# Attention with mixed heads and a gated feed-forward: gathers of score rows issued three places ahead instead of two

## The chip, the cores and the metric

One core of one Trainium2 chip runs the program. The metric is the device time of one execution in microseconds (us); for the kernel before there are three timed runs, and one more execution was recorded by the hardware profiler. All stretches named below are in us from the start of the profiled span.

## What is computed

Eight batches, 12 heads, 448 tokens, head size 64. The scores of all heads are mixed by a 12 x 12 matrix before the softmax, the weights are mixed by another behind it, and the result goes through a feed-forward stage with a gate. Cut to what matters:

```python
scores = scale * np.matmul(q, k.transpose(0, 1, 3, 2))        # (8, 12, 448, 448)
scores = np.einsum('bhij,hg->bgij', scores, w_pre)            # mix of heads
scores = scores - np.max(scores, axis=-1, keepdims=True)
attn = np.exp(scores)
attn = attn / (np.sum(attn, axis=-1, keepdims=True) + 1e-09)
attn = np.einsum('bhij,hg->bgij', attn, w_post)               # mix of heads
x = np.matmul(attn, v)                                        # to (8 * 448, 768)
h = x @ w_in                                                  # 768 -> 2048
out = (h - np.tanh(h)) @ w_out                                # 2048 -> 768
```

## The kernel before

**Blocks, groups, places.** A batch's 448 tokens are cut into blocks of 120, 120, 120 and 88 rows, 32 blocks in all. A block is cut into groups of 10 tokens or fewer, so that 10 tokens of 12 heads make up to 120 rows; there are 360 groups. Two groups make a *place* of the attention stage, of which there are 180, numbered from 0. The loop over places is at line 1256.

**What a place does on TensorE (PE), in this order.** `premix(p)` (line 910) mixes the heads of the scores of the place's two groups: eight matmuls at L918. Then come the place's *jobs* (below). Then `mix(p - 1)` (line 945), 32 matmuls at L957 that mix the heads of the softmax of the place before; they read `wr`, the mixing matrix divided by the row sums. `wr(p - 1)` comes from a chain over four engines: VectorE (DVE) takes the maximum (L927), ScalarE (ACT) the exponential with its sum (L929, twice), DVE the reciprocal (L938, L939, in `norm`, line 933), GpSimd (POOL) the product (L940). PE cannot go past `mix(p - 1)` before POOL has made that `wr`. (The counts are the profile's; the order below prints half of them, x4, x16 and x24 for L918, L957 and L999, since each of these matmuls runs as two.) ACT copies the result of a mix (`at`, L967 or L974) at the start of the next place.

**The gathers.** A block's scores lie in a tile `s` with a token to a partition. `gather(t)` (line 904) is a DMA on the SyncE queue (SP) that lays the rows of group `t` out as rows of `t`, one tile of a ring of `RT = 6`. At place p the loop issues the gathers of groups 2p + 4 and 2p + 5, those of place p + 2; the first four are issued ahead of the loop. A ring tile is free again once `premix` has read it.

**The jobs.** They prepare other blocks. `scores` (S below; line 864) makes two heads of a block's scores, 6 matmuls at L874 and two copies at L879, one on DVE and one on ACT; it comes in pairs, three pairs a block. `values` (V; line 987) multiplies three of six head pairs with v, 48 matmuls at L999. `prep_k` and `prep_q` (k, q; lines 806, 832) turn k and q by TensorE, split each into two parts on ACT (L825, L853) and DVE (L826, L855). A planner (lines 1153 to 1230) deals them out: the scores of the next block get a window of places from `lo` to `hi` (lines 1158, 1159) so that they are there before the first gather that reads them; values get a window of their own; `prep_k` takes the first place from four behind its load on that has no `prep_q` and not more than one scores job or two values jobs. Most places hold two S or one V; a place's jobs are sorted k, q, V, S.

**The conversion.** Beside this, the weights of the feed-forward are split into parts by `Convert` and `narrow_quad` (lines 35 and 72), 48 pieces in turn from place 7 on, a new one every three or four places, each in seven steps of one place. Its instructions stand at the head of a place on each engine, ahead of `norm` and so of `wr`. On POOL step 2 is one product (L84), step 4 two (L96, L97), step 5 some sums, step 6 a difference and a cast (L103, L105), step 7 another difference (L108). On DVE step 1 has L81 and L82, step 3 has L90, L91 and L94. In the second half of the pieces (`sums_out`, line 123, of `w_out`) the cast L105 waits for one more ACT product, L131, which stands on ACT behind the place's copy of `at`. Two pieces overlap, so a place can hold step 2 of one and step 6 of the one before.

**The DMA queue.** All loads, the gathers and the conversion's stores go out on SP in program order; `issue(6)` (line 769) sends up to six waiting entries a place behind the gathers. POOL issues DMAs only in the feed-forward stage, through a ring of descriptors in SBUF (`dynamic_dma_scratch_size`, line 1379).

The feed-forward follows from about 842 us on and is untouched but for that ring.

Of the kernel before, what the change touches and what calls it, by code (L numbers as in the profile page):

```python
# [150 lines left out]
def kernel_body(  # L151
# [11 lines left out]
    nc = tc.nc  # L163
# [72 lines left out]
    def open_ps_h():  # L236
        ff.ps_h = ctx.enter_context(tc.tile_pool(name="ps_h", bufs=2, space=PSUM, side="left"))
# [498 lines left out]
    with ExitStack() as st:  # L736
# [16 lines left out]
        blocks = [(b, m) for b in range(B) for m in range(NM)]  # L753
# [15 lines left out]
        def issue(most):  # L769
            for x in (queue, slow):  # L770
                while x and most and x[0][0] < place[0]:
                    send(x, nc.sync)
                    most -= 1
# [121 lines left out]

        RT = 6
        tq = [gp.tile([P, S], F32, name="t", tag=f"t{n}", bufs=1) for n in range(RT)]
        for x in tq:  # L900

# [2 lines left out]
        def gather(t, eng=nc.sync):  # L904
            i, g = groups[t]
            x = tq[t % RT]
            eng.dma_start(x[D - HP : D - HP + rows[t], :], sts[i][tokens[t].start : tokens[t].stop : tokens[t].step])
            tg[t] = x

        def premix(p):  # L910


            pss = [ps_p.tile([P, S], F32, name="ps_p", tag="ps_p") for _ in halves]
            ts = [tg.pop(2 * p + j) for j in range(2)]
            for j in (1, 0):
                for r in (1, 0):
                    k = slice(r * D, D + r * H * half_rows(2 * p + j)[r])
                    nc.tensor.matmul(pss[r][halves[j], :], wpre[k, :], ts[j][k, :], start=True, stop=True)  # L918
            return pss

        def expo(p, pss):
            zs = gp.tile([P, 3, 2], F32, name="zs", tag="zs")
            es = []
            for r, ps in enumerate(pss):

                mx = gp.tile([P, 1], F32, name="mx", tag="mx")
                nc.vector.tensor_reduce(out=mx, in_=ps, axis=AX.X, op=ALU.max, negate=True)  # L927
                e = gp.tile([P, S], F32, name="e", tag="e", bufs=4)
                nc.scalar.activation(e, ps, AF.Exp, bias=mx, scale=1.0, accum_out=zs[:, 0, r : r + 1])  # L929
                es.append(e)  # L930
            te[p] = [es, zs]

        def norm(p):
            zs = te[p][1]
            wr = gp.tile([P, 2, D], F32, name="wr", tag="wr", bufs=2)[:, :, :HP]
            for r in range(2):

                nc.vector.tensor_scalar_add(zs[:, 1, r : r + 1], zs[:, 0, r : r + 1], 1e-9)  # L938
            nc.vector.reciprocal(zs[:, 2], zs[:, 1])  # L939
            nc.gpsimd.tensor_mul(  # L940
                wr, wpost[:, :HP].unsqueeze(1).to_broadcast([P, 2, HP]), zs[:, 2].unsqueeze(2).to_broadcast([P, 2, HP])
            )
            te[p].append(wr)
# [203 lines left out]
        first = [t for t, (i, g) in enumerate(groups) if g == 0] + [NG, NG, NG]  # L1147
        todo = {p: [] for p in range(NPL + 8)}

        def at_place(p, *job):  # L1150
            todo[p].append(job)

        halved = []
        for i in range(len(blocks)):

            f0, f1, f2 = first[i : i + 3]
            if i + 1 < len(blocks):
                lo = max(0, (f0 - 1) // 2 - 1)
                hi = f1 // 2 - 3
                for x in range(0 if i else 1, 3):  # L1160
                    e = lo + 2 * x if lo + 4 <= hi else lo + (hi - lo) * x // 2
                    halved.append((e if i else x - 1, hi, "s", i + 1, x))
            for x in range(2):
                halved.append(((f1 - 1) // 2 + 2, f2 // 2 + 1 if f2 < NG else NPL + 7, "v", i, x))
        at_s, p, kind = {}, 0, None
# [22 lines left out]
        def held(p):  # L1188
            return [a for f, *a in todo[p] if f is scores]
# [11 lines left out]
        for i, (b, m) in enumerate(blocks):  # L1201
            p0 = first[i] // 2
            if i + 2 < len(blocks):
                p = at_s[i + 2, 0] - 1
# [5 lines left out]
                for hq in range(NP // 2):  # L1210
                    at_place(p0 + 4 + hq, load_v, b, hq)
        for b in range(1, B):
            p, o, done = first[blocks.index((b - 1, 1))] // 2 - 4, 0, []
            for hq in range(3):
                if hq == 2:

                    p = max(p, done[0] + 1)
                at_place(p, load_k, b, hq)
                o = max(p + 4, o + 1)
                p += 1  # L1220
                if hq > KB - 4:

                    o = max(o, end_s[blocks.index((b - 1, 3)), hq - 1 - (KB - 4)] + 1)
                for r in range(2):

                    while any(f is prep_q for f, *a in todo[o]) or 2 * len(held(o)) + sum(f is values for f, *a in todo[o]) > 2:
                        o += 1
                    at_place(o, prep_k, b, 2 * hq + r)
                done.append(o)
                assert o < at_s[blocks.index((b, 0)), hq], (b, hq)  # L1230
# [25 lines left out]
        for p in range(NPL + 3):  # L1256
            if mixed:
                mixed()
                mixed = None
            if 5 <= p < NPL + 1:  # L1260
                conv.place()
            place[0] += 1
            for t in (2 * p + 4, 2 * p + 5):
                if t < NG:
                    gather(t)
            issue(6)
            if p == NPL + 1:
                for f in start.pop(p):
                    f()
            if p < NPL:  # L1270
                ps = premix(p)
            if 1 <= p < NPL + 1:
                norm(p - 1)
            if p == NPL:
                for f in x0[1:]:
                    f()
            if p < NPL:
                expo(p, ps)
            if p > NPL:
                next(xq)  # L1280
                next(xq)
            for f, *a in todo[p]:
                f(*a)
            for f in sooner:
                f()
            sooner.clear()
            if 1 <= p < NPL + 1:
                mixed = mix(p - 1)
            for f in then + last:
                f()  # L1290
            then.clear()
            last.clear()
            if p == NPL - 3:
                conv.rest(now)
                early.close()
                open_early()
            if p == NPL - 1:
                early_ps.close()
                open_ps_h()
            for f in start.get(p, ()):  # L1300
                f()
            for _ in range(pieces.get(p, 0)):
                next(xl)
# [91 lines left out]
```

## Time and profile before

| | |
|---|---|
| three timed runs | 1706.41, 1708.94, 1719.01 us; median 1708.94 us |
| profiled execution | 1703.0 us, its span 1701.3 us |
| mean granted TensorE clock | 0.994 |
| attention, first `premix` to the last `mix` | about 25 to 842 us |
| DMA engines busy in the attention stage | 0.80 of the time |

The profile counts an engine busy while an instruction runs on it and names for each wait the engine or DMA whose signal came last. In rows of the timeline the columns are start, duration, engine, line, operation, output and inputs, and in brackets the idle time of the engine before it with the releaser. Only waits of the engine that sets the end cost time; in the attention stage that is PE, which is busy 97% of it, so the account is kept in PE's idle time and in the clock that it is granted.

### The profile page before, as it was taken

To read this page: it belongs to the slowest core of one execution; us is meant where nothing else is said; L and a number is where in the kernel's file an instruction comes from. 1 tells how busy PE (TensorE), PEld (TensorE's weight loads), DVE (VectorE), ACT (ScalarE), POOL (GpSimd) and SP (SyncE) were. 2 spreads that over 40 slices of the span, in tenths; PEclk is the share of its full clock that TensorE was granted. 3 is DMA by queue.
4 is the path that set the end of the run, shared out by engine and by line. 5 is a ranking of instruction groups with operands and counts; after the bars stand their busy time and mean duration, and the time that the engine had idled before them with its cause. 6 is when DMAs were issued, how large, how long until landed. Compare 5 with 4: busy or idle time off the path is not lost.

```text
span 1701.3 us, 41215 instructions
## 1 busy us (share of the span) xinstructions
PE 1660.1 (98%) x16068; PEld 1379.8 (81%) x16068; DVE 1231.3 (72%) x2119; ACT 1091.1 (64%) x1920; POOL 585.5 (34%) x798
## 2 busy tenths in 40 slices
PE   8999999999999899999999999999999999999999
PEld 6777777777777677677788888888888888989999
DVE  5777777878777777675497899868778867778432
ACT  5777777777777677676586777556667456666331
POOL 1466667666666666662100111101001101011100
PEclk9999999999999999999999999999999999999999
DMA  8879889898987979856589899989999989988993
GB/s 183 218 228 257 255 246 276 247 270 259 256 253 231 269 234 257 254 182 208 190 269 340 273 331 318 346 295 335 318 334 362 368 272 327 326 311 327 404 413 132
DMA packets 322290, 475.09 MB, mean 279 GB/s; under 512 B 105264, under 2 KB 255280, under 8 KB 322096
## 3 DMA queue, kind: packets, MB, share of 16 engines
q1 hardware_dynamic: 305660, 414.34, 75.5%
q0 software_dynamic: 16128, 57.68, 8.7%
q8 instruction: 128, 2.10, 0.5%
q14 instruction: 66, 0.54, 0.1%
q10 hardware_dynamic: 308, 0.43, 0.1%
HBM read 274.73 MB, written 120.59 MB: 232 GB/s over the span
## 4 chain that ended last, share of the span: by engine, by line
PE 72%; DMA 7%; DVE 7%; ACT 4%; issue 4%; POOL 4%; SPq 1%; POOLq 0%; ACTq 0%; DVEq 0%
PE ps_o L957 11%; PE ps_h L291 8%; PE ps_h L292 7%; PE ps_h L294 7%; PE ps_m L999 6%; PE ps_p L918 6%; PE y L534 6%; PE y L532 6%; PE y L533 6%; PE ps_q L874 4%; DMA t<-s 2%; DMA gl<-gs 2%; ACT e L929 1%; DVE mx L927 1%; PE y L504 1%
## 5 line engine op out<-in xcount | busy, mean ns | idle before, releaser
L957 PEld LDWEIGHTS ps_o<-wr,e 60*112 60x112 f32 (+1 forms) x5760 | 303.3, 175 | 46.1 <-POOL wr L940 31.9
L957 PE MATMUL ps_o<-wr,e 60*112 60x60 f32 (+1 forms) x5760 | 314.5, 259 | 16.1 <-POOL wr L940 14.6
L929 ACT ACTIVATE e<-ps_p,mx 128x448 f32<-128x448 f32 x360 | 224.8, 631 | 117.2 <-DVE mx L927 82.8
L927 DVE TENSOR_REDUCE mx<-ps_p 128x1 f32<-128x448 f32 x360 | 206.5, 615 | 109.1 <-PE ps_p L918 108.5
L967 ACT COPY at<-ps_o 112x960 f32<-112x960 f32 x156 | 154.3, 989 | 103.4 <-PE ps_o L957 102.9
L918 PE MATMUL ps_p<-t,wpre 60*64 60x448 f32 (+1 forms) x1440 | 182.4, 570 | 6.7 <-DMA t<-s 6.6
L999 PEld LDWEIGHTS ps_m<-at,vr 112*64 112x64 f32 x3072 | 147.6, 137 | 23.0 <-issue 7.7
L999 PE MATMUL ps_m<-at,vr 112*64 112x120 f32 (+1 forms) x3072 | 161.4, 262 | 1.1 <-DMA vr<-in_v_dram 0.9
L532 PE MATMUL y<-w,gh 128*128 128x384 f32 x448 | 151.2, 338 | 2.1 <-DMA w<-wo 1.6
L940 POOL TENSOR_TENSOR wr<-wpost,zs 128x120 f32<-128x120 f32 x180 | 70.0, 389 | 237.6 <-DVE zs L939 199.0
L533 PE MATMUL y<-w,gh 128*128 128x384 f32 x448 | 150.5, 336 | 0.0
L534 PE MATMUL y<-w,gl 128*128 128x384 f32 x424 | 143.4, 338 | 3.0 <-DVE gl L450 3.0
L874 PEld LDWEIGHTS ps_q<-kk,qh 64*120 64x120 f32 (+1 forms) x768 | 59.1, 174 | 82.0 <-issue 45.1
L874 PE MATMUL ps_q<-kk,qh 64*120 64x448 f32 (+1 forms) x768 | 121.8, 394 | 0.9 <-ACT kk L825 0.4
L879 DVE COPY s<-ps_q 120x448 f32<-120x448 f32 (+1 forms) x192 | 112.2, 614 | 9.8 <-PE ps_q L874 8.0
L669 POOL DMA_DIRECT2D gs<-gb x24 | 17.2, 717 | 291.6 <-DVE gb L668 291.6
L307 ACT ACTIVATE u<-h 128x1024 f32<-128x1024 f32 x56 | 59.5, 1063 | 74.4 <-DVE h L716 70.5
L879 ACT COPY s<-ps_q 120x448 f32<-120x448 f32 (+1 forms) x192 | 94.9, 538 | 7.1 <-PE ps_q L874 6.7
L647 POOL DMA_DIRECT2D gs<-ga x24 | 17.2, 716 | 230.0 <-DVE ga L330 222.9
L532 PEld LDWEIGHTS y<-w,gh 128*128 128x128 f32 x448 | 84.2, 188 | 7.2 <-issue 3.5
L533 PEld LDWEIGHTS y<-w,gh 128*128 128x128 f32 x448 | 84.1, 188 | 3.4
L534 PEld LDWEIGHTS y<-w,gl 128*128 128x128 f32 x424 | 79.6, 188 | 4.6 <-DVE gl L450 4.6
(372 smaller groups left out, 3971.3 us busy)
## 6 DMA issues: line engine op xcount, KB each, us to landing
t<-s SPq DMA_DIRECT2D x342, 210.0 KB
wa<-ss SPq DMA_DIRECT2D x96, 384.0 KB
w<-wo SPq DMA_DIRECT2D x43, 768.0 KB
gl<-gs SPq DMA_DIRECT2D x62, 512.0 KB
wa<-wi SPq DMA_DIRECT2D x72, 384.0 KB
w<-ts SPq DMA_DIRECT2D x35, 768.0 KB
gs<-gs POOLq DMA_DIRECT2D x24, 768.0 KB, 9.2
cr<-in_moe_w_in_dram SPq DMA_DIRECT2D x48, 256.0 KB
```

The costliest lines, as they stand in the source:

```text
L291: nc.tensor.matmul(ph, w[:, c, 0], xh, start=start and c == 0, stop=False, skip_group_check=True)
L532: nc.tensor.matmul(y, gh[:, tok], wh, start=first, stop=False, skip_group_check=True)
L533: nc.tensor.matmul(y, gh[:, tok], wl, start=False, stop=False, skip_group_check=True)
L534: nc.tensor.matmul(y, gl[:, tok], wh, start=False, stop=last, skip_group_check=True)
L874: nc.tensor.matmul(ps[:n, :S], qx[a, hp, :], kx[a, hp % 2], start=(x == 0), stop=(x == 2))
L879: eng(sts[i][:n, 2 * hp + j, :], ps[:n, :S])
L918: nc.tensor.matmul(pss[r][halves[j], :], wpre[k, :], ts[j][k, :], start=True, stop=True)
L927: nc.vector.tensor_reduce(out=mx, in_=ps, axis=AX.X, op=ALU.max, negate=True)
L929: nc.scalar.activation(e, ps, AF.Exp, bias=mx, scale=1.0, accum_out=zs[:, 0, r : r + 1])
L957: nc.tensor.matmul(ps[:CP, j, c * GP : (c + 1) * GP].rearrange("p (h i) -> p h i", i=GI)[:, :, r * GH : (r + 1) * GH], e[k, c * CP : (c + ...
L967: nc.scalar.copy(ats[i0][:, :, :, at : at + 2 * GI].rearrange("p c h (j i) -> p j (c h) i", j=2), ps[:CP, :, : NC * GP].rearrange("p j (x ...
L999: nc.tensor.matmul(pv[j * D : (j + 1) * D, r, :n], vt[:, j, c, :], ats[i][:, c, 2 * hp + j, :n], start=(c == 0), stop=(c == NC - 1),)
```

## The change

The ring gets eight tiles, and at place p the gathers of groups 2p + 6 and 2p + 7 go out, those of place p + 3; at place 0 four gathers go out, so that none is left out. The windows of the scores (`lo`, `hi`) and the loads of k move a place sooner, since a block's scores must now be complete a place sooner. The SBUF for two more tiles of 448 floats comes in part from POOL's descriptor ring, which is cut from 4096 to 2048 bytes a partition.

```diff
-        RT = 6
+        RT = 8
...
-                lo = max(0, (f0 - 1) // 2 - 1)
-                hi = f1 // 2 - 3
+                lo = max(0, (f0 - 1) // 2 - 2)
+                hi = f1 // 2 - 4
...
-            p, o, done = first[blocks.index((b - 1, 1))] // 2 - 4, 0, []
+            p, o, done = first[blocks.index((b - 1, 1))] // 2 - 5, 0, []
...
-            for t in (2 * p + 4, 2 * p + 5):
+            for t in range(2 * p + 6 if p else 4, 2 * p + 8):
                 if t < NG:
                     gather(t)
             issue(6)
...
-    nc = _bacc.Bacc("TRN2", target_bir_lowering=False, num_devices=1, dynamic_dma_scratch_size=4096)
+    nc = _bacc.Bacc("TRN2", target_bir_lowering=False, num_devices=1, dynamic_dma_scratch_size=2048)
```

No instruction is added but two MEMSETs of the new tiles (L902), which POOL runs at the start. The planner moves jobs between places, while the conversion stays at the same places: POOL's order is otherwise unchanged, and so is DVE's order of conversion steps against `norm`.

**PE, the k of the second load of a batch.** First the kernel before, places 17 and 18: `kr` is k as loaded, `kk` and `qh` the split k and q, `t` a ring tile, `ps_m`, `ps_q`, `ps_p`, `ps_o` PSUM tiles.

```order
L918 MATMUL ps_p<-t,wpre 64x448 x4
L814 MATMUL ps_m<-ident,kr 128x112 x8
L874 MATMUL ps_q<-kk,qh 120x448 x4
L874 MATMUL ps_q<-kk,ql 120x448 x2
L957 MATMUL ps_o<-wr,e 112x12x5 x16
L918 MATMUL ps_p<-t,wpre 64x448 x4
L874 MATMUL ps_q<-kk,qh 120x448 x4
L874 MATMUL ps_q<-kk,ql 120x448 x2
L957 MATMUL ps_o<-wr,e 112x12x5 x16
```

The same k in the changed kernel, places 16 and 17:

```order
L918 MATMUL ps_p<-t,wpre 64x448 x4
L814 MATMUL ps_m<-ident,kr 128x112 x8
L999 MATMUL ps_m<-at,vr 64x120 x24
L957 MATMUL ps_o<-wr,e 112x12x5 x16
L918 MATMUL ps_p<-t,wpre 64x448 x4
L874 MATMUL ps_q<-kk,qh 120x448 x4
L874 MATMUL ps_q<-kk,ql 120x448 x2
L874 MATMUL ps_q<-kk,qh 120x448 x4
L874 MATMUL ps_q<-kk,ql 120x448 x2
L957 MATMUL ps_o<-wr,e 112x12x5 x16
```

`prep_k` shared a place with one S and now shares one with V. Counted over PE's whole order within the loop, L814 is followed by scores in 10 places and by values in 11 before, and in 4 and 17 now. The places of the 10 are 17, 28, 40, 62, 73, 85, 107, 118, 130 and 152; of the 4 they are 5, 50, 95 and 140.

**ACT, the places with L131 directly ahead of L85** (step 6 of one piece of the second half beside step 2 of the next). There are five such places in each kernel, 99, 112, 125, 138 and 151. The second of them before, from the place's copy of `at` to the next place:

```order
L967 COPY at<-ps_o 112x2x48x10
L131 ACTIVATE ct<-ct 128x128
L85 ACTIVATE cr<-cr 128x512
L929 ACTIVATE e,zs<-ps_p,mx 128x448 x2
L974 COPY at<-ps_o 112x48x10
L974 COPY at<-ps_o 112x48x9
```

and in the changed kernel:

```order
L967 COPY at<-ps_o 112x2x48x10
L131 ACTIVATE ct<-ct 128x128
L85 ACTIVATE cr<-cr 128x512
L929 ACTIVATE e,zs<-ps_p,mx 128x448 x2
L879 COPY s<-ps_q 120x448
L974 COPY at<-ps_o 112x48x10
L974 COPY at<-ps_o 112x48x9
```

A copy of scores on ACT tells that the place now holds S where it held V (which leaves nothing on ACT). The five held, in their order, V with q, V, two S, V with q, two S; they now hold two S, S, S, two S, V with k.

## The prediction

> **What bounds the kernel now.** I read the busy time of the attention stage first, then PE's waits in it, then the timeline around each kind of wait.
>
> ```profile
> 25.20:842.00 816.80, 795.44 (x11596) 608.30 (x11596) 590.96 (x1502) 579.60 (x1329) 492.80 (x638) 0.99 0.80 240
> PE ps_o L957 <- POOL wr L940: 13.4, 16, 1.7
> PE ps_p L918 <- DMA t<-s: 6.6, 8, 1.6
> PE ps_m L999 <- DMA vr<-in_v_dram: 0.9, 1, 0.9
> ```
>
> The first row is the attention stage: 816.8 us, of them PE busy for 795.4 (the second number), DVE 591.0, ACT 579.6, POOL 492.8. PE sets the end, and only 21.4 us of the stage are left for any change of order to win. The other rows (us in total, times, longest) name nearly all of that: 6.6 us in which `premix` waited for its gathers, 13.4 us in which `mix` waited for POOL's `wr`. The change aims at the first, but it reorders the jobs that decide the second.
>
> **The gathers.** Why they are late shows on SP. The first rows are SP's own, the fifth is from the chain of waits, the last two are PE's.
>
> ```profile
> 155.91 1.62 SPq L907 DMA_DIRECT2D t<-s  x2
> 157.58 0.86 SPq L766 DMA_DIRECT2D kr<-in_k_dram  x1
> 158.61 6.68 SPq L766 DMA_DIRECT2D cr<-in_moe_w_in_dram  x2
> 165.39 1.65 SPq L907 DMA_DIRECT2D t<-s  x2
> 156.75 9.32 DMA t<-s
> 166.21 0.98 PE L918 MATMUL ps_p<-t,wpre 60*64 60x448 f32 x8 [0.93 <-DMA t<-s]
> 25.21 1.72 PE L918 MATMUL ps_p<-t,wpre 60*64 60x448 f32 x5 [1.65 <-DMA t<-s]
> ```
>
> A gather that went out at 156 took 9.32 us to land, and `premix` stood still for 0.93 us; SP itself hung for 6.68 us on two loads, so the next gathers were late too. A place lasts 816.8 / 180 = 4.54 us on average. Issued a place sooner, these gathers would have about 4.5 us more, against waits of under 1 us. The longest wait, 1.65 us, is that of place 0, whose gathers go out ahead of the loop as before; it stays. The gain is 6.6 - 1.65 = **-5.0 us**. SP sends the same DMAs in nearly the same mix, so what lies behind the gathers on its queue (loads with places to spare) is no later. The ring's own wait is the same too: with eight tiles the gather of place p + 3 needs the tile that `premix(p - 1)` read, as that of p + 2 did with six. A gather that opens a block still stands one place behind the last copies of its scores.
>
> The 0.9 us for `vr` is the last batch's v, read two places after its load; the values concerned now stand two places later (167 for 165), against a wait of 0.87 us: **-0.9 us**.
>
> **The k next to scores.** What PE loses to `wr` falls into kinds of places. The first kind is the place after `prep_k` and S.
>
> ```profile
> 100.01 1.16 DVE L826 TENSOR_TENSOR kk<-ps_m,kk 128x448 fp32r<-128x448 f32 x2 [0.46 <-ACT kk L825]
> 102.67 0.21 DVE L938 TENSOR_SCALAR zs<-zs 128x1 f32<-128x1 f32 x2
> 103.22 0.39 POOL L940 TENSOR_TENSOR wr<-wpost,zs 128x120 f32<-128x120 f32 x1 [3.54 <-DVE zs L939]
> 103.66 1.78 PE L957 MATMUL ps_o<-wr,e 60*112 60x60 f32 x32 [1.56 <-POOL wr L940]
> 153.33 1.78 PE L957 MATMUL ps_o<-wr,e 60*112 60x60 f32 x32 [0.99 <-POOL wr L940]
> 210.31 1.78 PE L957 MATMUL ps_o<-wr,e 60*112 60x60 f32 x32 [1.57 <-POOL wr L940]
> 358.31 1.79 PE L957 MATMUL ps_o<-wr,e 60*112 60x60 f32 x32 [0.65 <-POOL wr L940]
> 564.46 1.78 PE L957 MATMUL ps_o<-wr,e 60*112 60x60 f32 x32 [1.27 <-POOL wr L940]
> ```
>
> DVE is still at the split of k (1.16 us) when the place ends, then has step 3 of the conversion, and only then the reciprocal; `wr` is 1.56 us late. The five PE rows are the places after 17, 28, 40, 73 and 118, together 6.0 us. The other five such places (62, 85, 107, 130, 152) show no wait of this kind: no conversion step 3, or a place of two S behind, made the difference less. With V beside it a `prep_k` gives DVE 2.6 us more of PE time, and none of the 11 such places is followed by a wait. Now only four places hold k with S. Behind 51 and 96 there stand S and step 3, as in the two waits of 1.56 and 1.57, so I put 3.1 us there and nothing on the other two: -6.0 + 3.1 = **-2.9 us**. At places 18 and 41 two S with step 3 now follow two S; from nothing to half of the 1.56, I take 0.4 each, **+0.8 us**.
>
> **The conversion's cast next to scores.** This is the term that speaks against the change. In place 125:
>
> ```profile
> 589.64 0.98 ACT L967 COPY at<-ps_o 112x960 f32<-112x960 f32 x1
> 590.52 0.32 ACT L131 ACTIVATE ct<-ct 128x128 f32<-128x128 f32 x1
> 590.89 0.61 POOL L105 CAST ct<-ct 128x512 fp32r<-128x512 f32 x1 [1.61 <-ACT ct L131]
> 591.47 1.49 POOL L84 TENSOR_SCALAR cm<-cm 128x512 f32<-128x512 f32 x1
> 592.93 0.54 POOL L940 TENSOR_TENSOR wr<-wpost,zs 128x120 f32<-128x120 f32 x1
> 593.53 1.84 PE L957 MATMUL ps_o<-wr,e 60*112 60x60 f32 x32 [1.73 <-POOL wr L940]
> 719.56 1.78 PE L957 MATMUL ps_o<-wr,e 60*112 60x60 f32 x32 [1.62 <-POOL wr L940]
> 529.28 0.98 PE L918 MATMUL ps_p<-t,wpre 60*64 60x448 f32 x8
> 532.68 0.39 POOL L940 TENSOR_TENSOR wr<-wpost,zs 128x120 f32<-128x120 f32 x1
> 533.13 1.10 PE L957 MATMUL ps_o<-wr,e 60*112 60x60 f32 x18 [0.25 <-POOL wr L940]
> 590.35 0.63 PE L874 MATMUL ps_q<-kk,qh 64*88 64x448 f32 x4
> 591.43 0.37 PE L874 MATMUL ps_q<-kk,ql 64*88 64x448 f32 x2
> 688.05 1.79 PE L957 MATMUL ps_o<-wr,e 60*112 60x60 f32 x32 [0.62 <-POOL wr L940]
> ```
>
> The copy of `at` waits for the mix before; L131 stands behind it, POOL's cast waits for L131, the product L84 (1.49 us) follows, and `wr` comes last. So `wr` cannot be there sooner than some 3.85 us after the place's start (529.28 to 533.13 in place 112), whatever PE has to do. Place 112 holds V, which covers all but 0.25. Places 125 and 151 hold two S, done 2.3 us after the start: waits of 1.73 and 1.62. In 99 and 138, V with q covers it. One S (half of the two S of place 125, which run from 590.35 to 591.80, so 0.7 us, behind a `premix` of 0.9) is done at 1.6 and would leave 2.2. After the change 99 and 138 hold two S, 112 and 125 one S, 151 V with k: 2 x 1.7 + 2 x 2.2 = 7.8 us against 1.73 + 1.62 + 0.25 = 3.6, so **+4.2 us**. The bounds are nothing (were ACT's copy to come earlier) and 4 x 2.2 = 8.8 less 3.6.
>
> Without L84 in the place, the same chain made one S wait 0.62 us (688.05, place 145). S stands so at 119, 158 and 164 now, and at 145 no more: 3 x 0.62 - 0.62 = **+1.2 us**.
>
> **The clock.** Stalls of this length can cost twice.
>
> ```profile
> 591.71:595.12 3.41, 1.68 (x34) 1.59 (x32) 3.27 (x5) 1.74 (x6) 3.41 (x3) 1.00 1.01 242
> 595.12:598.53 3.41, 3.41 (x20) 1.78 (x18) 1.77 (x6) 1.70 (x5) 2.58 (x4) 0.50 0.88 293
> 718.00:721.41 3.41, 1.85 (x36) 1.79 (x40) 3.27 (x6) 1.54 (x6) 3.18 (x3) 1.00 0.87 281
> 721.41:724.82 3.41, 3.41 (x18) 1.74 (x18) 1.50 (x6) 2.05 (x4) 2.81 (x3) 0.50 1.11 262
> ```
>
> After 3.41 us with PE busy for 1.68 or 1.85 the next 3.41 us were granted half the clock (0.50), which costs up to 3.41 / 2 = 1.7 us. Both waits over 1.6 us did so, the waits of 1.56 and 1.57 did not. I expect three or four such drops in place of two, so 0 to +3.4, and take **+1.0**. The Trainium skill (TensorE: Matmul & The Clock Gate, "Why this matters for your kernels") wants no idle gaps of over about 3 us, a whole window, before the clock falls. By that rule no stall here would cost clock, this term would be 0 and the sum below -2.6 us; the trace disagrees, since 1.7 us of idleness within a window sufficed.
>
> **The smaller ring.** POOL's DMAs in the feed-forward:
>
> ```profile
> POOL gs L669 <- DVE gb L668: 291.6, 24, 16.5
> 957.29 0.75 POOL L670 DMA_DIRECT2D gs<-gs  x1
> 964.82 0.72 POOL L647 DMA_DIRECT2D gs<-ga  x1 [6.78 <-DVE ga L330]
> gs<-gs POOLq DMA_DIRECT2D x24, 768.0 KB, 9.2
> ```
>
> Three of them go out in some 18 us, each lands in 9.2 us or less, and POOL idles 6.8 us between them and 291.6 us for one line alone. Half a ring should hold what is in flight; should one DMA have to wait for an earlier one, POOL's idle time hides most of it. I take 0, with an upper end of 24 x (9.2 - 6.8) = 58 us. The Trainium skill (DMA: Bandwidth & Descriptors, "Terms") gives a descriptor 16 bytes, by which 2048 bytes make an estimated 128 descriptors an engine; no row here shows how many are in flight. The two added MEMSETs run on POOL while PE waits for the first loads: 0.
>
> **The sum.** -5.0 - 0.9 - 2.9 + 0.8 + 4.2 + 1.2 + 1.0 = -1.6 us. The same matmuls run, so PE's busy time stays. The profiled execution's 1703.0 becomes 1701.4; it lay 5.9 below the median of the timed runs, so for a median I forecast 1708.9 - 1.6 = **1707 us**: no change that a measurement tells (about 1%, 17 us, is what it can).
>
> **The rivals.**
>
> *Faster, 1699 us.* The gathers win their 5.0, and jobs that are spread more evenly (17 of the k beside V) remove the waits after k wholly, while the cast at the conversion costs as before, because ACT or POOL run ahead: -5.0 - 0.9 - 6.0 + about 2 = -10. For it: none of the 11 places of k with V was followed by a wait. Against it: the cast is bound to the mix before by L131, and POOL's order is fixed. If all 20 us of named waits but place 0's went, with two drops of the clock, the time would be 1709 - 22 = 1687.
>
> *Slower, 1718 us.* The cast next to scores decides: waits of 2.2 us at all of 99, 112, 125 and 138 (+5.2), 0.62 becoming 0.9 at the S without L84 (+2), the clock dropping after five stalls more (+8.5), less the 5.9 of gathers and v: +10. It is slower than before as soon as four drops are added. For it: both waits over 1.6 us halved the clock. Against it: where the stall lies across a window's edge it may not.
>
> *The gathers stay late*, 1712 us. If SP is held up by its loads for more than a place, as at 158.61 (6.68 us against 4.54), the extra place is used up and the 5.0 us are not won. Against it: waits of under 1 us need only that much more.
>
> *The ring stalls POOL*, 1730 us, some 20 of the 58 us.
>
> **Chances and range.** The forecast, within 6 us of 1707, 0.55; faster 0.18; slower 0.17; late gathers 0.06; the ring 0.04. The range runs from 1694 to 1719: it takes in the faster rival's middle and the slower one's, and leaves out its ends. Faster by over 1% (below 1692) needs nearly all waits gone: 0.06. Slower by over 1% (above 1726) needs the ring or more drops than I count: 0.07. Within 1%: 0.87.
>
> **What would show it.** In PE's waits `t<-s` falls from 6.6 us to about 1.7, the wait for `vr` goes; `wr` stays between 11 and 17 us, but at other places: waits of 1.6 us and more at the L957 that follow L131 and L84, at four places, most with S, one wait behind each of places 51 and 96, none after k with V. Windows at half clock stand behind the former. POOL's DMAs in the feed-forward keep 0.7 us. I am wrong if `t<-s` stays above 3 us, if `wr` falls below 8 us or rises above 22, or if the stage from 842 us on is more than 3 us longer.

## The result, and the profile after

Eleven runs of the changed kernel have a median of 1721.79 us (1715.43 to 1729.54), eleven of the kernel before on the same chip 1707.51 us (1702.51 to 1722.94): the ratio is 1.0072, 95% interval 1.0046 to 1.0098. The change costs some 12 us. The forecast was 1707, its range ended at 1719.

The profiled execution took 1726.18 us (span 1724.5, granted clock 0.986) against 1703.0 (1701.3, 0.994), 23.2 us more. The stretches first: of the changed kernel the attention stage and the feed-forward (columns as in the prediction's first row).

```profile
26.40:864.90 838.50, 810.40 (x11596) 617.00 (x11596) 592.23 (x1503) 581.66 (x1329) 493.98 (x638) 0.97 0.79 236
864.90:1724.50 859.60, 842.59 (x4328) 753.50 (x4328) 629.95 (x593) 501.77 (x573) 87.69 (x132) 1.00 0.89 318
```

The feed-forward before:

```profile
842.00:1701.30 859.30, 844.25 (x4328) 755.29 (x4328) 629.13 (x594) 501.70 (x573) 85.96 (x132) 1.00 0.89 319
```

The feed-forward has its old length (859.6 for 859.3). The attention stage is 838.5 - 816.8 = 21.7 us longer, and the busy column says of what kind: the same 11596 matmuls kept PE busy for 810.4 us in place of 795.4, so **15.0 us are slower matmuls**; PE's idle time went from 21.4 to 28.1, so **6.7 us are waits**. The remaining 1.2 us lie ahead of the first `premix`.

PE's waits in the attention stage of the changed kernel (us in total, times, longest):

```profile
PE ps_o L957 <- POOL wr L940: 26.1, 29, 2.2
PE ps_m L814 <- DVE s L879: 1.7, 2, 1.3
PE ps_p L918 <- DMA t<-s: 1.6, 1, 1.6
```

The gathers are there: 6.6 us have become the 1.6 of place 0, and the wait for `vr` is gone. But `wr`, 14.6 us over the same stretch before (the prediction's 13.4 stop at 842 us and leave out one wait of 1.16 us at the last mix, which both kernels have), is at 26.1, and a kind of wait that did not exist is there too (L814 for copies of scores).

Next the clock. These are windows of the changed kernel behind places 112, 138 and 158; the number behind POOL's is the granted clock.

```profile
546.40:549.81 3.41, 1.25 (x12) 0.59 (x10) 2.53 (x5) 2.87 (x8) 2.71 (x4) 0.99 0.64 232
549.81:553.22 3.41, 3.41 (x36) 3.20 (x40) 2.03 (x5) 0.29 (x1) 2.66 (x3) 0.50 0.24 83
553.22:556.64 3.42, 3.42 (x26) 1.95 (x18) 1.73 (x4) 1.96 (x7) 1.76 (x2) 0.51 0.38 131
...
672.54:675.95 3.41, 1.82 (x20) 1.01 (x12) 2.84 (x6) 3.38 (x9) 2.63 (x4) 1.00 1.20 257
675.95:679.37 3.42, 3.42 (x60) 2.65 (x62) 2.82 (x7) 0.98 (x1) 2.67 (x3) 1.00 0.82 236
...
771.60:775.01 3.41, 2.63 (x43) 2.13 (x40) 3.38 (x9) 2.37 (x7) 2.74 (x4) 1.00 0.75 261
775.01:778.43 3.42, 3.42 (x20) 1.81 (x20) 2.80 (x7) 1.90 (x5) 3.26 (x4) 0.50 0.53 182
```

In the first window PE was idle for 2.16 us, and two windows at half the clock follow, although PE was busy throughout both. Behind place 138 it was idle for 3.41 - 1.82 = 1.59 us and nothing followed; behind 158 for 0.78, and the clock fell. Behind place 0, whose wait of 1.65 us costs a window in both kernels, and up to the end of the stage the trace has 12 windows at half clock, in eight lots; before it had 3, each by itself. Nine more at up to 1.7 us are 15 us, which is what the busy column shows. It is no accident of this execution: over all runs the mean granted clock is 0.9863, against 0.9917 over 29 runs of the kernel before (those beside the first four experiments). A window at half clock loses up to half its length, so the clock's part of the time is about 1721.8 x 0.0137 - 1708.8 x 0.0083 = 23.6 - 14.2 = 9.4 us of the median's 14.3. In two other sets of runs the kernel before stood at 0.9896 (1709.02 and 1710.52 us), so this is good to some 4 us.

The cast next to scores came as forecast; place 125 now, with one S:

```profile
609.52 0.32 ACT L131 ACTIVATE ct<-ct 128x128 f32<-128x128 f32 x1
609.90 0.61 POOL L105 CAST ct<-ct 128x512 fp32r<-128x512 f32 x1 [1.71 <-ACT ct L131]
610.48 1.50 POOL L84 TENSOR_SCALAR cm<-cm 128x512 f32<-128x512 f32 x1
612.39 1.78 PE L957 MATMUL ps_o<-wr,e 60*112 60x60 f32 x32 [2.18 <-POOL wr L940]
```

The chain is the one that the prediction read in the old place 125, one S shorter on PE: 2.18 us for its 2.2. Two waits that it did not name:

```profile
54.22 0.43 DVE L81 TENSOR_SCALAR cm<-cr 128x512 f32<-128x512 f32 x1 [3.34 <-DMA cr<-in_moe_w_in_dram]
...
691.23 6.67 SPq L766 DMA_DIRECT2D wo<-co  x1
705.51 1.15 DVE L879 COPY s<-ps_q 88x448 f32<-88x448 f32 x2 [3.27 <-DMA t<-s]
706.18 0.98 PE L814 MATMUL ps_m<-ident,kr 112*128 112x112 f32 x8 [1.35 <-DVE s L879]
```

In place 7 DVE stands 3.34 us at the first conversion load, with the reciprocal behind it, and `wr` is 2.14 us late. Around place 145 SP hangs for 6.67 us on a store, so the last gathers of an old tile `s` go out late; DVE's copy of new scores into that tile waits 3.27 us for them, and PE 1.35 us for DVE.

### The profile page after: what moved, and what is told of

Same layout as the page of the kernel before. It is cut to its first block, busy times and chain, and to the rows that moved or that the text cites. A ratio compares the mean times of both kernels' runs of the same rounds, so it can differ in the third digit from the quotient of the medians.

```text
span 1724.5 us, 41200 instructions
## 1 busy us (share of the span) xinstructions
PE 1674.4 (97%) x16068; PEld 1387.9 (80%) x16068; DVE 1233.4 (72%) x2119; ACT 1093.2 (63%) x1920; POOL 589.3 (34%) x800
## 4 chain that ended last, share of the span: by engine, by line
PE 70%; DMA 8%; DVE 7%; issue 5%; ACT 4%; POOL 4%; SPq 1%; DVEq 0%; POOLq 0%; ACTq 0%
PE ps_o L957 11%; PE ps_h L294 7%; PE ps_h L291 7%; PE ps_h L292 7%; PE ps_m L999 6%; PE y L532 6%; PE y L534 6%; PE y L533 6%; PE ps_p L918 6%; PE ps_q L874 4%; DMA t<-s 2%; DMA w<-wo 1%; DMA gl<-gs 1%; ACT e L929 1%; PE ps_m L840 1%
## 5 line engine op out<-in xcount | busy, mean ns | idle before, releaser
L957 PEld LDWEIGHTS ps_o<-wr,e 60*112 60x112 f32 (+1 forms) x5760 | 308.1, 177 | 60.0 <-POOL wr L940 45.3
L957 PE MATMUL ps_o<-wr,e 60*112 60x60 f32 (+1 forms) x5760 | 320.0, 261 | 27.1 <-POOL wr L940 26.1
L874 PE MATMUL ps_q<-kk,qh 64*120 64x448 f32 (+1 forms) x768 | 125.8, 405 | 1.2 <-DVE kk L826 0.5
```

Source lines behind the costliest of these rows:

```text
L874: nc.tensor.matmul(ps[:n, :S], qx[a, hp, :], kx[a, hp % 2], start=(x == 0), stop=(x == 2))
L957: nc.tensor.matmul(ps[:CP, j, c * GP : (c + 1) * GP].rearrange("p (h i) -> p h i", i=GI)[:, :, r * GH : (r + 1) * GH], e[k, c * CP : (c + ...
```

## The experiments

The theory (A in the expectations): the planner's new order puts scores into places where `wr` is late anyway, and the loss is mostly the clock behind those stalls. The rival (B): the deeper gathers themselves cost, by what they push on SP or by copies that wait for them. Every kernel was timed beside the kernel before on the same chip; the windows at half clock are those of the profiled execution in the attention stage, without the one that stands behind place 0 in nearly every trace and those at the last mix.

| kernel | median us | ratio to before, 95% interval | mean clock of the runs | windows at half clock |
|---|---|---|---|---|
| the change | 1721.79 | 1.0072 (1.0046 to 1.0098) | 0.9863 | 12 |
| planner's part alone | 1735.01 | 1.0151 (1.0124 to 1.0178) | 0.9850 | 13 |
| gathers and ring alone | 1708.64 | 0.9996 (0.9979 to 1.0013) | 0.9907 | 7 |
| change, L131 first | 1712.01 | 1.0020 (1.0002 to 1.0038) | 0.9898 | 11 |
| change, PE kept busy | 1712.19 | 1.0026 (1.0007 to 1.0045) | 0.9956 | 1 |
| before, wr on DVE | 1747.88 | 1.0217 (1.0189 to 1.0244) | 0.9867 | 7 |
| change, wr on DVE | 1770.44 | 1.0345 (1.0311 to 1.0378) | 0.9777 | 25 |
| change, k's number at 4 | 1725.33 | 1.0082 (1.0053 to 1.0111) | 0.9875 | 11 |
| before, conversion behind | 1730.32 | 1.0109 (1.0078 to 1.0141) | 0.9837 | 14 |
| change, conversion behind | 1718.50 | 1.0049 (1.0024 to 1.0074) | 0.9920 | 8 |
| change, both cures | 1705.39 | 0.9967 (0.9946 to 0.9989) | 0.9953 | 4 |
| before, both cures | 1704.15 | 0.9969 (0.9947 to 0.9991) | 0.9940 | 3 |
| change, both cures, two loads a place | 1738.34 | 1.0157 (1.0127 to 1.0186) | 0.9822 | 11 |
| before, both cures, two loads a place | 1759.40 | 1.0276 (1.0245 to 1.0307) | 0.9787 | 21 |

### The two halves of the change

The planner's part alone, on the kernel before:

```diff
-                lo = max(0, (f0 - 1) // 2 - 1)
-                hi = f1 // 2 - 3
+                lo = max(0, (f0 - 1) // 2 - 2)
+                hi = f1 // 2 - 4
...
-            p, o, done = first[blocks.index((b - 1, 1))] // 2 - 4, 0, []
+            p, o, done = first[blocks.index((b - 1, 1))] // 2 - 5, 0, []
```

> The kernel before with the planner's part of the change alone: scores' products and the loads of k a place sooner, gathers two places ahead into six tiles, ring of 4096. Theory A (the new order of jobs puts one or two S beside the conversion's cast, the stalls of 1.6 us and more halve the clock for windows of 3.41 us): as slow as the change or somewhat slower, 1720 to 1728 us; PE's waits for wr about 26 us up to 842 us, for the gathers up to 6 us, eight or more windows at half clock. Theory B (the deeper gathers themselves cost, by what they put ahead of the loads on SP or by copies that wait for a late gather of an old tile): about 1707 us, three windows as before.

Its waits:

```profile
PE ps_o L957 <- POOL wr L940: 21.4, 28, 2.2
PE ps_p L918 <- DMA t<-s: 8.1, 6, 3.1
PE ps_m L814 <- DVE s L879: 7.8, 4, 3.5
```

The loss is here, and more than all of it: +26 us, above the 1720 to 1728 that A gave. `wr` rose by 6.8 us over the kernel before, which A had asked for. The gathers, two places ahead as ever, now cost 8.1 us themselves, and 7.8 us are copies of scores that wait for them, which A had not: the copies moved a place sooner and the gathers did not.

The other half, gathers and ring with the old table of jobs:

```diff
-        RT = 6
+        RT = 8
...
-            for t in (2 * p + 4, 2 * p + 5):
-                if t < NG:
-                    gather(t)
             issue(6)
...
             for f in sooner:
                 f()
             sooner.clear()
             if 1 <= p < NPL + 1:
                 mixed = mix(p - 1)
...
+            for t in range(2 * p + 6 if p else 4, 2 * p + 8):
+                if t < NG:
+                    gather(t)
...
-    nc = _bacc.Bacc("TRN2", target_bir_lowering=False, num_devices=1, dynamic_dma_scratch_size=4096)
+    nc = _bacc.Bacc("TRN2", target_bir_lowering=False, num_devices=1, dynamic_dma_scratch_size=2048)
```

> The kernel before with eight tiles, the ring of 2048 and gathers three places ahead, but the planner's table of jobs as it was. So that a gather stays behind the copies of its scores, it is issued at the end of a place and not in its middle. Theory A: faster by the gathers' 5.0 us, about 1702 us; wr near 14.6 us, t<-s about 1.7 us, about three windows at half clock. Theory B: the loss is here, about 1720 us, with twelve windows.

```profile
PE ps_o L957 <- POOL wr L940: 13.9, 16, 1.6
PE ps_p L918 <- DMA t<-s: 5.1, 7, 1.7
```

Neither A's 1702 nor B's 1720. No loss (0.9996), so B falls as the main cause, and the ring of half the size costs nothing. No gain either: `t<-s` is at 5.1 and not at 1.7. Issued at the end of place p these gathers stand behind the loads of that place on SP, so part of the extra place is gone; that this is why was not tested. Its trace also holds the price of bad luck: one wait of 1.6 us at place 18 was followed by four windows at half clock in a row.

### The cast, and the clock by itself

ACT's product for the cast is issued ahead of the copy of `at`:

```diff
+DUE = []
...
-    done = sums(nc, m, t[:, :, 1])
+    DUE.append(sums(nc, m, t[:, :, 1]))
     yield
     nc.gpsimd.tensor_sub(ol, m, raw(oh))
-    done()
...
+            while DUE: DUE.pop(0)()
             if mixed:
-                mixed()
-                mixed = None
+                mixed = mixed()
```

> The whole change, but ACT's product of the conversion (L131) is issued ahead of the place's copy of at (L967), so that POOL's cast (L105) no longer waits for the mix before. Theory A: the waits at places 99, 112, 125 and 138 (7.6 us in all) and the windows at half clock behind them go; wr falls from 26 to about 18 us, four to five windows fewer, 1708 to 1712 us. Theory B: 1722 us, as the change.

```profile
PE ps_o L957 <- POOL wr L940: 17.9, 27, 2.0
PE ps_m L814 <- DVE s L879: 6.8, 3, 4.5
```

`wr` fell from 26.1 to 17.9, and the time by 9.8 us to 1712.0, as A said. The waits at 99, 112 and 138 are gone, at 125 one of 1.6 is left (L84 still stands ahead of `wr`); that is 6.0 us of the 8.2, the rest is other places. The windows did not fall by four in this execution (11): three stand behind copies of scores that waited 2.0 and 4.5 us for gathers (places 33 and 145), and three behind waits at 51 and 68 that are as long in the change and cost no clock there. Over the runs the clock did rise, to 0.9898.

Then no wait is taken away, but PE gets something to do in it: 54 matmuls (the expectation says 56) into the bank that `mix` overwrites.

```diff
+        FILL = {7: 7, 28: 3, 29: 3, 51: 5, 96: 7, 99: 5, 112: 7, 125: 7, 138: 5, 146: 5}
...
             ps = ps_o.tile([P, 2, 512], F32, name="ps_o", tag="ps_o")
+            busy(FILL.get(p + 1, 0), ps[:, 0])
```

> The whole change plus matmuls of 128x128 (3 to 7 at a place, 56 in all; their result is overwritten by the mix that follows) in the ten places with the longest waits for wr, ahead of the mix. They take none of the waits away, they only keep PE busy in them. If the clock is what a stall costs: six or more of the twelve windows at half clock go and the time falls by 8 to 12 us, to about 1711. If the stalls' own length or the deeper gathers are the cost: 1722 us or a little more.

```profile
PE ps_o L957 <- POOL wr L940: 12.2, 29, 1.2
```

More work, and 9.6 us less time (1712.19). One window at half clock is left of twelve, and the clock is at 0.9956, above that of the kernel before. The mixes begin no sooner for it: place 51 lasts 5.06 us for 5.08, place 125 5.66 for 5.65. What went is the clock's part, which the prediction put at 1.0 us. By the reckoning above the clock's part fell from 23.6 to some 7.5 us, by more than the 9.6 us of the medians, so either the windows cost less than half their length over the runs, or some 6 us were lost elsewhere; no trace shows which. The two profiled executions differ by 16.4 us (1726.18 and 1709.83).

### wr on another engine

One word, on the kernel before and on the change:

```diff
-            nc.gpsimd.tensor_mul(
+            nc.vector.tensor_mul(
                 wr, wpost[:, :HP].unsqueeze(1).to_broadcast([P, 2, HP]), zs[:, 2].unsqueeze(2).to_broadcast([P, 2, HP])
```

> The kernel before with one word changed: wr (L940) is computed on DVE, right behind its reciprocal, and not on POOL, so the conversion's products and casts on POOL no longer stand ahead of it. If POOL's queue is what wr waits for at the cast: the waits at places 125 and 151 (3.4 us) go, all others get some 0.4 us shorter (no hand-over to POOL), wr falls from 14.6 to 6 to 9 us, two to three windows at half clock fewer: 1698 to 1703 us. If DVE, which gets 180 x 0.2 us more, becomes late instead: 1709 us or more.

> The whole change with wr (L940) on DVE in place of POOL. If POOL's queue at the conversion's cast is what the new order of jobs ran into: the waits at 99, 112, 125 and 138 (7.6 us) go wholly, those behind k with S (51, 96) get shorter, wr falls from 26 to about 10 us, six or more windows at half clock go, and the gathers' 5 us show at last: 1698 to 1704 us, no slower than the kernel before with the same word changed. If the deeper gathers cost something of their own (copies of scores that wait for a late gather): some 5 to 10 us slower than that kernel.

1747.88 and 1770.44 us: what the first expectation hoped for failed and its other branch came (DVE late, 1709 us or more), and the second failed in both its branches. `wr` is at 34.0 and 43.1 us. The instruction's line on the kernel before with DVE (ns, least/median/longest) and a place of it:

```profile
L940 DVE TENSOR_TENSOR wr<-wpost,zs x180: 282/284/1398, 30.7 to 881.9; 128x120 f32<-128x120 f32 x180
```

```profile
108.60 1.29 POOL L96 TENSOR_TENSOR cm<-cr,co 128x512 f32<-128x512 f32 x1 [1.88 <-DVE zs L938]
108.82 1.20 DVE L940 TENSOR_TENSOR wr<-wpost,zs 128x120 f32<-128x120 f32 x1
```

The product takes 0.28 us by itself and 1.20 here, where it ends just behind POOL's product, which had begun first; the mix behind it waited 2.70 us. Of its 180 instances 99 overlap an instruction of POOL and take 0.70 us on average; the 81 others take 0.285 at the most. The Trainium skill (SBUF — State Buffer, "SBUF: two separate sides") says that a DVE operation with two SBUF inputs and one of GpSimd shut each other out for a whole instruction; this trace agrees. So the wait was not taken from POOL's queue but carried into DVE's, with the maxima and the copies behind it. The pair still tells one thing: with `wr` on DVE the change is again slower than the kernel before, by 22.6 us, with 25 windows at half clock for 7. It is not POOL's queue alone that the new order runs into.

### The k put back, and the conversion behind

The change with the number in L1213 at 4 again:

```diff
-            p, o, done = first[blocks.index((b - 1, 1))] // 2 - 5, 0, []
+            p, o, done = first[blocks.index((b - 1, 1))] // 2 - 4, 0, []
```

> The whole change but with the k planned where they were (the number in L1213 back to 4); scores, gathers, tiles and ring as changed. If the scores' places alone bring the loss (one or two S beside the cast at 99, 112, 125, 138): 1718 to 1726 us, as the change, with wr between 24 and 30 us. If the k's places bring it: 1708 to 1712 us.

```profile
PE ps_o L957 <- POOL wr L940: 26.0, 27, 2.8
PE ps_m L814 <- DVE s L879: 5.7, 2, 3.4
```

1725.33 us, with `wr` at 26.0, as the expectation had it for the scores' places. The edit did not put the k back where they were, though: the planner now has seven with S (6, 28, 51, 73, 96, 118, 141), for ten before and four in the change, and five of the places behind them wait 6.8 us in all, not counting place 7. The waits at the cast stay (7.4 us at the four places). So loading k a place sooner is not by itself what costs; how much of the rest is due to the scores' places this run does not tell apart.

Then the conversion's step of a place goes behind `norm` and `expo`, on both kernels:

```diff
-            if 5 <= p < NPL + 1:
-                conv.place()
             place[0] += 1
...
                 expo(p, ps)
+            if 5 <= p < NPL + 1: conv.place()
```

> The kernel before with the conversion's step of a place issued behind the place's norm and expo instead of ahead of its premix, so that no step of it stands ahead of wr on POOL or of the reciprocal on DVE. If it is the conversion ahead of wr that PE waits for: wr falls from 14.6 to below 5 us, no window at half clock inside the attention, 1695 to 1700 us. If the steps only push the maxima and exponentials of the next place back: 1709 us or more.

> The whole change with the conversion's step of a place issued behind norm and expo. If the change lost its time by putting scores beside conversion steps that stand ahead of wr: wr from 26 to below 8 us, the gathers' 5 us show, 1692 to 1700 us, no slower than the kernel before with the same edit. If places of scores alone are too short for what DVE, ACT and POOL have to do in them anyway: 10 us or more slower than that kernel.

The kernel before with it, then the change with it:

```profile
PE ps_o L957 <- POOL wr L940: 10.4, 14, 1.2
PE ps_p L918 <- DMA t<-s: 9.2, 7, 2.2
```

```profile
PE ps_o L957 <- POOL wr L940: 11.2, 17, 1.2
PE ps_m L814 <- ACT s L879: 4.4, 2, 3.3
PE ps_m L840 <- DVE s L879: 4.0, 6, 2.2
```

`wr` fell in both, to 10.4 and 11.2, not to below 5 and 8, and nothing was won by it: PE now waits for gathers (9.2 us) in the one and for copies of scores, which stand behind the conversion's steps, in the other (8.4 us). 1730.32 us, the first expectation's other branch (1709 or more), and 1718.50, far from the expected 1700 and less. Of the second expectation only the end holds: with the conversion there the change is no slower than the kernel before. That fits a loss of this order of jobs against that order of conversion steps, and not of places of scores as such; but both kernels got new waits by the edit, so it is not shown.

### Both cures together

L131 first, and matmuls into the waits that were left, on both kernels (the edit of L131 as above):

```diff
+        FILL = {7: 7, 28: 3, 29: 3, 51: 5, 68: 3, 96: 7, 125: 5, 158: 2}
```

> The whole change with L131 ahead of the copy of at, and 2 to 7 overwritten matmuls (35 in all) ahead of the mix in the eight places that still waited then. The two cures together: no waits at 99, 112 and 138, and hardly a window at half clock left: granted clock 0.995 or more, 1701 to 1706 us. If clock and stalls do not add up: 1710 us or more.

```diff
+        FILL = {18: 5, 29: 3, 41: 5, 74: 2, 101: 2, 119: 4, 125: 5, 146: 3}
```

> The kernel before with the same two cures (L131 ahead of the copy of at; 29 overwritten matmuls in the eight places that waited for wr). Its few windows at half clock go: clock 0.995 or more, 1701 to 1704 us. With clock and cast out of the way on both sides the change should then stand within 3 us of the kernel before: its gathers won 5 us, its own waits cost some 3 to 6.

The change with the cures:

```profile
PE ps_o L957 <- POOL wr L940: 9.6, 23, 1.2
PE ps_m L814 <- DVE s L879: 7.0, 3, 3.8
```

The kernel before with them:

```profile
PE ps_o L957 <- POOL wr L940: 4.5, 11, 1.2
PE ps_p L918 <- DMA t<-s: 4.4, 5, 1.6
PE ps_m L999 <- DMA vr<-in_v_dram: 3.8, 4, 1.6
```

1705.39 us, as expected, and 1704.15, at the end of what was expected but with a clock of 0.9940 for the 0.995; both are below the kernel before (0.9967 and 0.9969). Of the change's 14.3 us against it 1.2 are left, inside the intervals. These are the two fastest kernels of the study; between them nothing is decided. The gathers still win their part (2.1 us for 4.4, and no wait for v), and it goes to `wr` (9.6 for 4.5) and to copies that wait for gathers (7.0 for nothing).

### Why those gathers are late

The change with both cures, around place 145:

```profile
681.18 0.73 SPq L766 DMA_DIRECT2D kr<-in_k_dram  x1
682.87 7.39 SPq L766 DMA_DIRECT2D wo<-co  x1
690.36 2.06 SPq L907 DMA_DIRECT2D t<-s  x2
```

A load of v, one of k and a store of the conversion fall into one place, SP hangs on the third, and the next gathers go out 7 us late. So at most two a place, on both kernels:

```diff
-            issue(6)
+            issue(2)
```

> The whole change with both cures (L131 ahead of the copy of at, 35 overwritten matmuls), and at most two queued loads or stores a place on SP where it was six: where a load of k, one of v and a store of the conversion fell into one place (about 155 and 681 us), the third goes a place later, behind the next gathers. If the gathers were late because SP stood for 6.9 to 7.4 us behind such a third DMA: PE's waits for the copies of scores (7.0 us at L814) fall below 3 us, and the time by about 4, to 1700 to 1702 us. If they were late for another reason: 1705 us.

> The kernel before with both cures and at most two queued loads or stores a place on SP. Its copies of scores never waited for gathers, so only t<-s (4.4 us) and the waits for v (3.8 us) can get shorter or, as v goes out later, longer: 1702 to 1706 us. If the kernel above then stands 2 us or more below this one, the deeper gathers are worth their place once nothing else stands in the way.

PE's waits in the change with it, then DVE's:

```profile
PE ps_o L957 <- POOL wr L940: 27.8, 27, 6.8
```

```profile
DVE co L90 <- DMA wi<-co: 15.9, 3, 9.0
DVE co L90 <- DMA wo<-co: 7.9, 3, 3.5
```

PE's waits in the kernel before with it:

```profile
PE ps_o L957 <- POOL wr L940: 52.2, 28, 10.3
```

The times failed (1738.34 and 1759.40 us): stores of the conversion go out late now, its step 3 on DVE waits for their buffers, 23.8 us in the change and 25.4 + 25.0 = 50.4 in the kernel before, and `wr` stands behind it. What was asked is answered all the same: the waits for copies of scores are gone, 7.0 us to none, and even the kernel before, two places ahead, waits for gathers only at place 0 (1.6 us). A gather is late here by what goes out ahead of it on SP.

The third DMA is not why SP hangs, though. With two a place SP hangs on the gather that takes the third one's turn, at 153.88 (for 5.93 of the 6.75 us of two gathers):

```profile
151.75 1.62 SPq L766 DMA_DIRECT2D kr<-in_k_dram  x1
153.88 6.75 SPq L907 DMA_DIRECT2D t<-s  x2
```

The gain is that the second of these two gathers went out 7.0 us after its place (29) began, for 11.7 us. In the fifteen traces SP stood for over 5 us on one DMA 75 times in the attention stage, on loads, stores and gathers, and each time the DMA just ahead was a load of k, 75 of 315 such loads. Why is not shown. The last sentence of the second expectation holds by the letter (the change stands 21 us lower), but the two differ in how many stores were late, so it tells nothing of the gathers.

## Why the prediction was wrong

**The step that failed is the clock**: "Stalls of this length can cost twice", of which it took +1.0 us. The mechanism was right and stood in the prediction with its rows; the size was off by a factor of nine (the runs' mean clock) to fifteen (the profiled execution's busy time). Of the 15.9 us between the forecast change (-1.6) and the measured one (+14.3), some 8 are this term; most of the rest is `wr`, which rose by 11.5 us for the forecast 3.3 (below). The clock's term failed in three ways. First, it took 1.6 to 1.7 us of waiting as the bound, having looked only behind the longest waits. But that kernel had a third drop inside the stage, behind place 146:

```profile
690.69:694.10 3.41, 2.43 (x42) 1.97 (x38) 2.51 (x10) 1.93 (x6) 3.20 (x5) 1.00 0.84 277
694.10:697.51 3.41, 3.41 (x20) 1.52 (x20) 1.22 (x3) 2.75 (x6) 3.15 (x4) 0.50 1.14 255
```

0.98 us of idleness sufficed there, which could have been read before. Counted window by window in all fifteen traces, no window in which PE was idle for less than 0.78 us was followed by a drop, each of the 35 with 1.7 us or more was, and of those between 63 of 150 were: 8 of 53 up to 1.0 us, 55 of 97 above.

Second, it counted the drops at the cast alone. There the count came out: three lots, behind 99, 112 and 125. The other five stand behind places 7, 29, 96, 146 and 158, waits of 2.14, 0.94, 2.21, 1.61 and 0.78 us, of which the sum had only 1.56 at 96 and 0.62 at 158. Without place 0 and the last mix, windows in which PE is idle for 1 us or more are nine in the stage now and were four before.

Third, it priced a drop at one window; on average there were one and a half. That could not be read before, since each of the three drops there was one window long. The kernel with PE kept busy shows the size of the whole: 9.6 us back with no wait removed.

**The other terms, in the prediction's order.**

- The gathers, -5.0: 6.6 to 1.6. Right. That the ring's own wait stays the same: right. That nothing else on SP is harmed: not so. The prediction followed the gathers and what they wait for, and not who waits for the gathers: the copies of the next scores into the tile that they read. These now cost 1.7 us directly, in other runs of the same order up to 7.0.
- The wait for `vr`, -0.9: gone. Right.
- The k next to scores, -2.9: 1.58 us at 51 and 2.21 at 96 for the expected 1.56 each. But "none after k with V" failed: 1.03, 0.42 and 1.61 us at places 28, 118 and 146, each a single S behind a k with V, 3.1 us in all. At 146:

```profile
711.28 1.16 DVE L826 TENSOR_TENSOR kk<-ps_m,kk 128x448 fp32r<-128x448 f32 x2 [1.36 <-ACT kk L825]
714.79 1.39 PE L957 MATMUL ps_o<-wr,e 60*112 60x60 f32 x24 [1.61 <-POOL wr L940]
```

The place begins at 711.43, so DVE's split of k runs into it in spite of V's longer time on PE. All 11 places of k with V before had two S behind them, which covered this. The 6.0 us of the old kind gave way to 6.9, so the term was +0.9 and not -2.9.
- Places 18 and 41, +0.8: no wait there. Wrong by that.
- The cast next to scores: 1.64, 2.16, 2.18 and 1.60 us, 7.6 for the expected 7.8. Right, and confirmed by L131 moved first (6.0 us less at these places).
- S without L84: 0.60, 0.78 and 0.67 us at 119, 158 and 164 for 0.62 each. Right.
- The ring, 0: the feed-forward is as long as it was, and half the ring at the old order costs nothing (0.9996). Right.

- The MEMSETs, 0: right. The first `premix` began 1.2 us later, but in two experiments with the same MEMSETs at 25.2 and 25.4, as before. It goes with the clock: the trace before has the full clock from 4.6 us on, that of the change from 7.0.

**What was not counted.** By these terms `wr` should have risen by 3.3 us, to about 18; it reached 26.1. The 8.2 us between are place 7 (2.1, DVE at the first conversion load), the three places behind k with V (3.1), places 29 and 68 (0.94 each) and thirteen waits of 0.18 to 0.43 us (4.4), against 3.2 us that the kernel before had outside the named kinds. At 29 and 68 it is step 4: POOL's two products (at 68 of 1.48 and 1.35 us) end just as `wr` begins, and PE has one S. About half of the thirteen are places with a single S too, of which there are 39 now for 32. The prediction looked up the places that it knew to be dear, and did not ask what an S alone costs next to every other step. Its own bound said that it was wrong if `wr` rose above 22 us.

**The rivals.** The slower one named the right mechanism ("the clock dropping after five stalls more", 1718 us) and was given 0.17; its argument against itself, that a stall across a window's edge may not count, is true of place 51 (0.91 and 0.66 us idle in two windows, no drop) and not of place 7 (1.05 and 1.09, a drop); at 138 a wait within one window cost nothing either. Its "slower than before as soon as four drops are added" is a slip: its own +5.2, +2 and -5.9 are above nothing with no drop at all. That the gathers stay late and that the ring stalls POOL did not happen.

What stays open: why between 0.8 and 1.7 us of idleness some windows cost the clock and others not, and why half clock lasts one window after some stalls and three or four after others, with PE busy in all of them.

## What to carry to other kernels

Where PE is busy 97% of a stage, cost a reordering by what it does to the clock: add up PE's idle time window by window, count each window that is idle for 1.7 us or more as one or two windows at half clock, and those from 1.0 to 1.7 at about half of that, not only those behind the longest waits. A few matmuls whose result is overwritten, put into a wait that can't be removed, got back 9.6 us here, as much as shortening the chain behind four of the waits. When a transfer is issued sooner, look at who waits for the buffer that it reads, and at what else stands ahead of it on its queue.

## What the runs showed of the hardware

- The clock: a drop comes in windows of 3.41 us, behind one in which PE was idle for 0.78 to 1.7 us (63 of 150) or longer (35 of 35), and can last for up to four windows in which PE never stopped (behind the one wait of 1.6 us at place 18, gathers and ring alone). The Trainium skill (TensorE: Matmul & The Clock Gate, "What's actually happening") has the window and the half clock, but asks for a whole idle window; these traces do not.
- DVE and POOL: a DVE product of 0.28 us takes 0.70 on average and up to 1.40 where POOL is at work.
- SP can hang for 5 to 7.8 us on a single load, store or gather that goes out just behind a load of k (75 times in fifteen traces; behind any other DMA 3.9 us at the most); everything behind it on the queue is that much later.
